# A routed-attention and tanh-shrink kernel on one core: order of the sums' product, of the weight checks, of the first two pairs and of the last flag, and how memory is handed over

## The chip, the cores and the metric

One core of a Trainium2 chip runs the whole program in one launch. The metric is the device time of one execution in microseconds (us), the median of the runs; lower is better. The engines are PE (TensorE, matrix products), DVE (VectorE), ACT (ScalarE) and POOL (GpSimd); SP only issues DMAs and waits. Every engine works through its own instructions in order and waits on semaphores for the others. A PE row in the trace gives matmuls; PEld rows are the weight loads beside them.

## The reference, cut to what matters

```
q, k, v: (4, 8, 768, 64) f32;  centroids: (8, 16, 64);  w_in: (512, 2048) f64;  w_out: (2048, 512) f64
assign  = argmax over 16 centroids of the normalised row . normalised centroid   (for q and for k)
scores  = q k^T / 8, kept only where q and k have the same cluster
attn    = exp(scores - max) / (sum + 1e-9);   x = attn v, heads side by side -> (3072, 512)
h = x w_in;   g = h - tanh(h);   out = g w_out          -> (3072, 512) f32
```

## The kernel before, in words

**Attention.** The 4 batches have 8 heads each, worked on in 16 pairs of heads (`pairs`, four to a batch, HP = 4). A pair is loaded (`load`: q, k and v on SP's queue), transposed (`turn`: PE into a PSUM tile, copied out by ACT or DVE), compared with the centroids (`similar`), given cluster codes (`route`, five DVE steps around a PE transpose), and its q codes go through DRAM (`publish`) to come back spread over the partitions (`spread`). Each pair has two halves of 384 queries, and each half has three steps (NS = 3) of two key tiles. A step is `score` (PE product, then ACT exp in PSUM), `select` (DVE: keep the exps whose codes match, tile `e`), and `value` (PE product into the PSUM tile `av`). `select` also lets POOL add the `e` tiles up into `sum` (L350, L354), except in the first half of the four pairs of batch 0, where PE does it (`early`).

**End of a half.** After the third step `total` (L383) multiplies `sum` by ones on PE (the sums' product, tile `den`, L391), has ACT copy `av` to `xT` (L396) and `den` to SBUF (L398), and POOL add it into `wholes` (L399). `divide` (three calls) makes the reciprocal on DVE (L405), multiplies `xT` by it (L408) and lets POOL add it into `inverses` (L409).

**Projections.** Batch 0 is projected by `plain_items` while its second halves and batch 1 are attended to. Batches 1 to 3 use a seven-product Strassen scheme (`strassen_items`): eight `up_pair` items (seven short PE products each, L595, DVE adds between, ACT tanh, POOL subtracts) and 21 `down_product` items (L637). Its factors are made once, kept in DRAM and streamed in by SP (`stream`, L536). While batch b+1 is attended to, batch b is projected; batch 3's items stand after the loop as the tail.

**Weights.** They come as 64-bit words. `weights_on` fetches a piece by POOL's queue and rounds it to f32 (ACT L120, DVE L121, L125, L128). Because the rounding holds only for values of some size, each half piece is read again later (`check_on`, SP, L728) and DVE reduces it to its least magnitude (`check_done`, L738): 64 checks.

**Order.** `steps` (L679) lists 96 attention steps. The loop emits for a step, in this order: the next pair's `similar`, `spread`, the next step's scores (`begin`), this step's `value`, at the end of a half `total`, and then the projection items of this step, in whose places (`between`) the list `todo` is spread out: the next step's selects, `turns`, divides, weight rounding, `route`, `publish`, the checks. Some steps have no item of their own: then all of `todo` is emitted at once; below these are called bare steps. In the Strassen stages the steps of a half are: a step with an `up_pair`, a bare step, a step with an `up_pair`.

**Memory.** `open_late` (L540) closes the pools of the first stages (weights, `g`, output and raw tiles) and opens the late ones on the same memory, among them `stream`, before step 48.

**End.** After the tail the checks, `wholes` and `inverses` become one flag (L854 to L868: six DVE steps, a PE transpose `pl`, a DVE reduction), which all engines load (L1017); a general path would follow if it were 0.

Of the kernel before, what the change touches and what calls it, by code (L numbers as in the profile page):

```python
# [30 lines left out]
F32 = mybir.dt.float32  # L31
# [7 lines left out]
P = 128  # L39
# [14 lines left out]
def kernel(  # L54
# [10 lines left out]
    nc = tc.nc  # L65
# [64 lines left out]
    def fast():  # L130
# [51 lines left out]
        def centroid_load():  # L182
            nc.scalar.dma_start(cen, centroids.rearrange("h c d -> (h c) d"))
# [128 lines left out]
        def spread(n: int, half: int):  # L312

            t = rows[n, half] = qbp.tile([P, 2, TB], BF16, name="row")
            nc.sync.dma_start(
                t.rearrange("p h n -> p (h n)"),
                q_codes[n][half].rearrange("h j p -> (h j p)").unsqueeze(0).to_broadcast([P, 2 * TB]),
            )
# [60 lines left out]
        def early(n: int, half: int):  # L379

            return n < HP and half == 0

        def total(n: int, half: int):  # L383

            b, p = pairs[n]
            s = sums.pop((n, half))
            ps = s
            if not early(n, half):
                ps = ps_f.tile([P, TB], F32, name="den", tag="f")
                for h in range(2):  # L390
                    nc.tensor.matmul(  # L391
                        ps[h * D : h * D + D], lhsT=ones, rhs=s[:, h], start=True, stop=True
                    )
            if half == 0:
                xT[n] = xp.tile([P, 2, TB], F32, name="xT")
            nc.scalar.copy(out=xT[n][:, half], in_=avs.pop((n, half)))  # L396
            t = dens[n, half] = sump.tile([P, TB], F32, name="den")
            nc.scalar.activation(out=t, in_=ps, func=ACT.Copy, bias=EPS)  # L398
            nc.gpsimd.tensor_tensor(out=wholes, in0=wholes, in1=t, op=ALU.add)  # L399
# [140 lines left out]
        def open_late():  # L540
            first.close()
            for name, bufs in (
                ("g", 1), ("diff", 1), ("u", 2), ("s", 2), ("th", 2), ("left", 1), ("du", 1), ("c", 4),
                ("stream", 3), ("raw", 1),
            ):
                late_pools[name] = cx.enter_context(tc.tile_pool(name=name + "_late", bufs=bufs))
            late_pools["G"] = late_pools["g"].tile([P, HF, 2, 2, TB], F32, name="G")
            late_pools["S1"] = late_pools["left"].tile([P, HF, TB], F32, name="S1")
            for n in range(2):
                fetch_factors(n)  # L550
# [192 lines left out]
        def begin(step):  # L743
            n, half, s = step
            for i in range(2):
                score(n, half, 2 * s + i)

        load(0)
        centroid_load()
        constants()  # L750
        for i in range(3):
            fetch()
        load(1)
        load(0, (2,))
        load(1, (2,))
        for n in range(2, HP):
            load(n, (0, 1, 2))
        turn(0, 0, nc.scalar)
        turn(0, 1, nc.vector)
        centroid_norms()  # L760
        similar(0)
        turn(1, 0, nc.scalar)
        route(0)
        publish(0)
        spread(0, 0)
        weights_on()
        begin(steps[0])
        weights_on()
        for i in range(2):
            select(*steps[0][:2], i)  # L770
        turn(1, 1, nc.scalar)
        similar(1)
        route(1)
        publish(1)


        fills = {HALF: (lambda: plain_items(0), HALF), 2 * HALF: (lambda: plain_items(1), 2 * HALF)}
        for b in range(1, B - 1):
            fills[2 * (b + 1) * HALF] = (lambda b=b: strassen_items(b), 2 * HALF)

        late, makers = [], []
        fill, whole, spent, since, over = [], 0.0, 0.0, 0, 1
        for at, (n, half, s) in enumerate(steps):
            b, p = pairs[n]
            following = steps[at + 1] if at + 1 < len(steps) else None
            after = steps[at + 2] if at + 2 < len(steps) else None
            if at == 4 * HALF:
                open_late()
            if at in fills:
                fill, over = fills[at][0](), fills[at][1]  # L790
                whole, spent, since = sum(it[0] for it in fill), 0.0, at
            if at == 2 * HALF:
                makers = [it for i in range(2) for it in up_maker(i)]
                makers += [it for i in range(2) for it in down_maker(i)]
            now = []
            part = (at - since + 1) / over
            while fill and (spent + fill[0][0] / 2 <= whole * part or part == 1):
                now.append(fill.pop(0))
                spent += now[-1][0]
            stages = ready.get(at, {})  # L800
            if 1 in stages:
                stages[1]()
            if after and after[2] == 0:
                spread(*after[:2])
            if following:
                begin(following)
            value(n, half, s)
            if s == NS - 1:
                total(n, half)
                late += [lambda n=n, half=half, i=i: divide(n, half, i) for i in range(HCH)]  # L810
                if half == 1:
                    load(n + (HP if n < 2 else 2), (2,) if n < 2 or n >= HP else ())

            todo = []
            if following:
                todo += [lambda i=i: select(*following[:2], 2 * following[2] + i) for i in range(2)]
            if 0 in stages:
                todo.append(stages[0])
            todo += late
            late = []  # L820
            todo += [weights_on] * (3 if HALF <= at < 2 * HALF else 1)
            if makers:
                share = -(-len(makers) // max(4 * HALF - 2 - at, 1))
                todo += makers[:share]
                makers = makers[share:]
            todo += [stages[i] for i in (2, 3) if i in stages]
            if late_pools:
                todo = [check_done] + todo + [check_on]
            slots = max(sum(it[1] for it in now), 1)
            place = iter(range(slots))  # L830

            def between():
                i = next(place)
                for it in todo[i * len(todo) // slots : (i + 1) * len(todo) // slots]:
                    it()

            if at in fills and late_pools:
                right_factors(b - 1)
            for it in now:
                it[2](between)  # L840
            if not now:
                between()
        for it in late:
            it()
        right_factors(B - 1)
        for it in strassen_items(B - 1):
            place = iter(range(9))
            it[2](lambda: (check_done(), check_on()) if next(place) == 0 else None)
        while waiting or (words == 2 and checked < 2 * len(PIECES)):
            check_done()  # L850
            check_on()


        for t, bound in ((inverses, MOST_INVERSE), (wholes, SUM_MOST)):  # L854
            nc.vector.tensor_scalar(out=t, in0=t, scalar1=bound, scalar2=None, op0=ALU.is_le)
# [10 lines left out]
        pl = ps_a.tile([1, P], F32, name="pl", tag="a")  # L866
        nc.tensor.transpose(out=pl, in_=fine, identity=ident)
        nc.vector.tensor_reduce(out=flag, in_=pl, axis=AX.X, op=ALU.min)  # L868


    def general():
# [180 lines left out]
```

## Time and profile before

| | |
|---|---|
| median of 3 runs (lowest, highest) | 1120.57 us (1119.27, 1124.29) |
| the profiled execution | 1122.21 us, its span 1120.4 us |
| mean granted TensorE clock | 0.971 |
| busy: PE, DVE, POOL, ACT | 91%, 55%, 49%, 27% of the span |

The profile comes from one execution; its span runs from the first to the last instruction of the program. A row of a timeline has the start in us, the duration in us, the engine, the line, the operation, the tiles as out<-in, and in square brackets how long the engine was idle before it and what ended that. A granted clock of 1.00 is TensorE's level of 2.4 GHz and 0.50 its level of 1.2 GHz; values between are stretches that hold both.

### The profile page before, as it was taken

How to read it: one execution, taken by the hardware profiler on the slowest of the kernel's cores; microseconds unless marked ns; L12 is line 12 of the kernel's file. 1: busy time of each engine (PE TensorE's matmuls, PEld its weight loads, DVE VectorE, ACT ScalarE, POOL GpSimd, SP SyncE). 2: the span in 40 equal slices, each digit the busy share in tenths (PEclk: the TensorE clock that was granted, in tenths of full speed). 3: DMA queues.
4: the chain of work that ended last, by engine and by line, in shares of the span. 5: the costliest groups of instructions: out<-in, count | busy, mean ns of one | idle time of the engine just before them, and what ended most of it. 6: DMA issues, size and time to landing. Idle time of an engine off the chain costs nothing.

```text
span 1120.4 us, 12005 instructions
## 1 busy us (share of the span) xinstructions
PE 1018.7 (91%) x4258; PEld 566.6 (51%) x4258; DVE 618.5 (55%) x1100; ACT 299.7 (27%) x458; POOL 552.9 (49%) x398
## 2 busy tenths in 40 slices
PE   3776999899999997889889999998889999999996
PEld 2332444344444442445446666544446766556885
DVE  3578899425776765465654544664635544544112
ACT  2343434213333332332223121222333121122000
POOL 1012354334545554475658634566668644356701
PEclk9888999999999999899999999999999999999998
DMA  9232354104244343423323343422332233334520
GB/s 226 75 106 78 90 170 134 45 17 120 77 129 135 122 158 104 131 78 109 114 92 122 116 129 124 128 90 94 87 134 95 94 115 104 122 127 138 191 99 31
DMA packets 101603, 124.68 MB, mean 111 GB/s; under 512 B 55328, under 2 KB 80928, under 8 KB 98848
## 3 DMA queue, kind: packets, MB, share of 16 engines
q1 hardware_dynamic: 94576, 100.73, 29.3%
q0 software_dynamic: 6816, 23.07, 6.3%
q8 instruction: 36, 0.59, 0.2%
q14 instruction: 31, 0.25, 0.1%
q10 hardware_dynamic: 144, 0.03, 0.0%
HBM read 102.79 MB, written 21.02 MB: 111 GB/s over the span
## 4 chain that ended last, share of the span: by engine, by line
PE 73%; DVE 11%; POOL 8%; DMA 3%; issue 3%; ACT 2%; SPq 0%; DVEq 0%; POOLq 0%; ACTq 0%
PE pu L595 19%; PE pd L637 19%; PE sc L327 9%; PE av L363 9%; PE o L437 7%; PE h L422 4%; POOL sum L354 4%; POOL G L586 3%; DVE e L341 2%; PE pt L248 2%; PE den L391 2%; PE sim L267 2%; DVE den L405 1%; DVE w_out L125 1%; PE den L372 1%
## 5 line engine op out<-in xcount | busy, mean ns | idle before, releaser
L354 POOL TENSOR_TENSOR sum<-sum,e 128x768 f32<-128x768 f32 x112 | 210.5, 1879 | 111.1 <-DVE e L341 106.9
L341 DVE SCALAR_TENSOR_TENSOR e<-row,code,sc 128x384 f32<-128x384 bf16 x384 | 211.5, 606 | 92.3 <-ACT sc L332 75.0
L332 ACT ACTIVATE sc<-sc 128x768 f32<-128x768 f32 x192 | 145.2, 790 | 255.9 <-PE sc L327 245.0
L637 PE MATMUL pd<-stream,G 128*128 128x256 f32 x864 | 193.3, 382 | 1.4 <-POOL G L586 1.4
L637 PEld LDWEIGHTS pd<-stream,G 128*128 128x128 f32 x864 | 162.3, 190 | 35.9 <-issue 9.6
L327 PE MATMUL sc<-t,t 64*128 64x384 f32 x768 | 160.5, 530 | 19.1 <-DVE e L341 16.4
L595 PE MATMUL pu<-xT,stream 128*128 128x384 f32 x384 | 145.7, 518 | 7.0 <-DMA stream<-up_factors 7.0
L363 PE MATMUL av<-e,vals 128*64 128x384 f32 x768 | 148.6, 509 | 0.0
L327 PEld LDWEIGHTS sc<-t,t 64*128 64x128 f32 x768 | 67.9, 191 | 96.0 <-issue 61.1
L586 POOL TENSOR_TENSOR G<-G,th 128x768 f32<-128x768 f32 x48 | 87.3, 1836 | 54.8 <-ACT th L585 54.8
L595 PEld LDWEIGHTS pu<-xT,stream 128*128 128x128 f32 x384 | 76.2, 202 | 68.5 <-issue 22.4
L595 PE MATMUL pu<-diff,stream 128*128 128x384 f32 x288 | 101.7, 486 | 0.8 <-DVE diff L561 0.8
L405 DVE RECIPROCAL den<-den 128x128 f32<-128x128 f32 x96 | 84.0, 918 | 18.0 <-POOL wholes L399 18.0
L363 PEld LDWEIGHTS av<-e,vals 128*64 128x64 f32 x768 | 47.5, 139 | 90.5 <-issue 89.4
L422 PE MATMUL h<-xT,w_in 128*128 128x384 f32 x256 | 88.4, 495 | 1.5 <-ACT den L398 1.3
L437 PE MATMUL o<-w_out,g 128*128 128x512 f32 x192 | 88.8, 610 | 0.0
L585 ACT ACTIVATE th<-G 128x768 f32<-128x768 f32 x48 | 39.4, 841 | 164.7 <-DVE G L581 164.7
L399 POOL TENSOR_TENSOR wholes<-wholes,den 128x384 f32<-128x384 f32 x32 | 31.8, 994 | 90.5 <-ACT den L398 90.5
L350 POOL TENSOR_TENSOR sum<-e 128x768 f32<-128x768 f32 x28 | 50.6, 1808 | 47.9 <-DVE e L341 47.9
L595 PEld LDWEIGHTS pu<-diff,stream 128*128 128x128 f32 x288 | 54.3, 190 | 38.3 <-DVE diff L561 1.4
L581 DVE TENSOR_TENSOR G<-pu,s 128x384 f32<-128x384 f32 x24 | 13.4, 557 | 105.8 <-PE pu L595 105.8
L653 POOL DMA_DIRECT2D out_dram<-c x36 | 19.9, 554 | 99.2 <-DVE c L648 96.9
(100 smaller groups left out, 913.9 us busy)
## 6 DMA issues: line engine op xcount, KB each, us to landing
stream<-up_factors SPq DMA_DIRECT2D x24, 896.0 KB, 5.5
stream<-down_factors SPq DMA_DIRECT2D x21, 1024.0 KB, 4.9
raw<-in_moe_w_in_dram POOLq DMA_DIRECT2D x16, 512.0 KB, 4.2
raw<-in_moe_w_out_dram POOLq DMA_DIRECT2D x16, 512.0 KB, 4.6
again<-in_moe_w_in_dram SPq DMA_DIRECT2D x32, 256.0 KB, 3.8
again<-in_moe_w_out_dram SPq DMA_DIRECT2D x32, 256.0 KB, 4.2
x<-in_q_dram SPq DMA_DIRECT2D x32, 192.0 KB, 5.7
x<-in_k_dram SPq DMA_DIRECT2D x32, 192.0 KB, 4.2
```

Source lines behind the costliest of these rows:

```text
L327: nc.tensor.matmul(sc[:, h, 0:TB], lhsT=turned[n, 1][r].rearrange("p a n -> p (a n)")[:, j * P : (j + 1) * P], rhs=turned[n, 0][r, half], ...
L332: nc.scalar.activation(out=sc[:, :, 0:TB], in_=sc[:, :, 0:TB], func=ACT.Exp, scale=SCALE)
L341: nc.vector.scalar_tensor_tensor(out=e[:, h], in0=rows[n, half][:, h], scalar=codes[n][:, 1, j // HCH, h, j % HCH : j % HCH + 1], in1=sc[: ...
L350: nc.gpsimd.tensor_tensor(out=s, in0=pair[:, 0], in1=pair[:, 1], op=ALU.add)
L354: nc.gpsimd.tensor_tensor(out=s, in0=s, in1=pair[:, i], op=ALU.add)
L363: nc.tensor.matmul(avs[n, half][h * D : h * D + D], lhsT=vals[n][:, h, j], rhs=e[:, i, h], start=(j == 0), stop=(j == NCH - 1),)
L405: nc.vector.reciprocal(out=t[:, c], in_=t[:, c])
L422: nc.tensor.matmul(h, lhsT=w_in[i][:, c, o * P : (o + 1) * P], rhs=xT[c][:, half], start=(c == 0), stop=(c == CD - 1),)
L437: nc.tensor.matmul(acc[sub], lhsT=gs[f % HF][:, f // HF, sub * P : (sub + 1) * P], rhs=w_out[f // FQ][:, f % FQ], start=(f == sequence[0]) ...
L586: nc.gpsimd.tensor_tensor(out=g[:, f].rearrange("p a n -> p (a n)"), in0=g[:, f].rearrange("p a n -> p (a n)"), in1=th.rearrange("p a n -> ...
L595: nc.tensor.matmul(ps, lhsT=streams[base + i][:, k_, c], rhs=right[which][c], start=(c == 0), stop=(c == CH - 1),)
L637: nc.tensor.matmul(ps, lhsT=left[:, i], rhs=t[:, i], start=(i == 0), stop=(i == HF - 1))
```

## The change

1. `total` is split. `take` has ACT copy `av` right after `value`. `total` itself (the sums' product, its copy, the POOL add) goes into `todo`, behind the selects and the turns, and the three divides into the next step's `todo`. The last pair of a batch keeps the old order in its second half (in batch 0 in both).
2. The two halves of a check part company: each step's `todo` now ends with two `check_done` and two `check_on`, where it began with one `check_done` and ended with one `check_on`. The late `raw` pool has 2 buffers for 1. The tail has no checks any more.
3. The late pools are opened with `reuse_waits="tile"`, so that a tile waits for the old tiles on whose memory it lies and not for the whole of the old pools.
4. Before the loop, pairs 0 and 1 are both transposed, routed and published, with four weight pieces rounded between them, where two were rounded and pair 1 followed the first selects; the loads of pairs 2 and 3 are emitted in another order, the centroids' load first, and the centroid norms before the second transpose.
5. The flag is made after the first two items of the tail, and the other items follow it.

```diff
+        def take(n: int, half: int):
+            if half == 0:
+                xT[n] = xp.tile([P, 2, TB], F32, name="xT")
+            nc.scalar.copy(out=xT[n][:, half], in_=avs.pop((n, half)))
+
         def total(n: int, half: int):
...
-            if half == 0:
-                xT[n] = xp.tile([P, 2, TB], F32, name="xT")
-            nc.scalar.copy(out=xT[n][:, half], in_=avs.pop((n, half)))
             t = dens[n, half] = sump.tile([P, TB], F32, name="den")
...
-                ("stream", 3), ("raw", 1),
+                ("stream", 3), ("raw", 2),
             ):
-                late_pools[name] = cx.enter_context(tc.tile_pool(name=name + "_late", bufs=bufs))
+                late_pools[name] = cx.enter_context(
+                    tc.tile_pool(name=name + "_late", bufs=bufs, reuse_waits="tile")
+                )
...
+        centroid_load()
         load(0)
-        centroid_load()
         constants()
         for i in range(3):
             fetch()
         load(1)
         load(0, (2,))
+        load(2)
         load(1, (2,))
+        load(3)
         for n in range(2, HP):
-            load(n, (0, 1, 2))
+            load(n, (2,))
         turn(0, 0, nc.scalar)
+        centroid_norms()
+        weights_on()
         turn(0, 1, nc.vector)
-        centroid_norms()
         similar(0)
+        weights_on()
         turn(1, 0, nc.scalar)
         route(0)
+        turn(1, 1, nc.scalar)
         publish(0)
         spread(0, 0)
+        similar(1)
         weights_on()
+        route(1)
         begin(steps[0])
+        publish(1)
         weights_on()
         for i in range(2):
             select(*steps[0][:2], i)
-        turn(1, 1, nc.scalar)
-        similar(1)
-        route(1)
-        publish(1)
...
             if s == NS - 1:
-                total(n, half)
-                late += [lambda n=n, half=half, i=i: divide(n, half, i) for i in range(HCH)]
+                take(n, half)
+                divides = [lambda n=n, half=half, i=i: divide(n, half, i) for i in range(HCH)]
+
+                if p == HP - 1 and (half == 1 or b == 0):
+                    total(n, half)
+                    late += divides
+                    divides = []
...
             todo += late
             late = []
+            if divides:
+                todo.append(lambda n=n, half=half: total(n, half))
+                late, divides = divides, []
...
             if late_pools:
-                todo = [check_done] + todo + [check_on]
+                todo += [check_done, check_done, check_on, check_on]
...
         right_factors(B - 1)
-        for it in strassen_items(B - 1):
-            place = iter(range(9))
-            it[2](lambda: (check_done(), check_on()) if next(place) == 0 else None)
-        while waiting or (words == 2 and checked < 2 * len(PIECES)):
-            check_done()
-            check_on()
-
+        tail = strassen_items(B - 1)
+        for it in tail[:2]:
+            it[2](lambda: None)
...
         nc.vector.tensor_reduce(out=flag, in_=pl, axis=AX.X, op=ALU.min)
+        for it in tail[2:]:
+            it[2](lambda: None)
```

## Rows read from the trace of the kernel before

**Rows 1.** The page's first part: busy time, share of the span, instructions.
```profile
PE 1018.7 (91%) x4258; PEld 566.6 (51%) x4258; DVE 618.5 (55%) x1100; ACT 299.7 (27%) x458; POOL 552.9 (49%) x398
```
**Rows 2.** Stages: length; busy PE, PEld, DVE, ACT, POOL; granted clock; DMA share, GB/s.
```profile
130.00:200.00 70.00, 63.23 (x230) 30.10 (x228) 66.38 (x104) 28.04 (x49) 33.38 (x30) 1.00 0.44 135
440.00:588.00 148.00, 126.70 (x486) 63.48 (x484) 80.20 (x150) 40.38 (x60) 85.13 (x58) 0.94 0.35 110
```
**Rows 3.** Waits of the whole run: total us, how often, the longest.
```profile
PE den L391 <- POOL sum L354: 20.6, 10, 3.3
PE sc L327 <- DVE e L341: 16.4, 16, 3.2
DVE smallest L738 <- DMA again<-in_moe_w_in_dram: 42.8, 11, 11.9
```
**Rows 4.** Timeline of a bare step and the half's end, and a later half's end.
```profile
495.08 1.58 ACT L585 ACTIVATE th<-G 128x768 f32<-128x768 f32 x2 [7.18 <-DVE G L581]
498.74 1.97 PE L327 MATMUL sc<-t,t 64*128 64x384 f32 x8 [0.82 <-DVE e L341]
505.42 0.91 PE L391 MATMUL den<-sum,ones 128*64 128x384 f32 x4 [3.27 <-POOL sum L354]
...
954.13 0.87 PE L391 MATMUL den<-sum,ones 128*64 128x384 f32 x4 [0.85 <-POOL sum L354]
```
**Rows 5.** Chain of waits, three whole up_pair items: start, duration, what.
```profile
471.80 10.92 PE pu L595 x28
...
542.12 9.23 PE pu L595 x28
...
833.75 10.92 PE pu L595 x28
```
**Rows 6.** Granted clock just behind the wait at 502 us (columns of group 2).
```profile
505.40:510.00 4.60, 4.58 (x11) 2.34 (x12) 0.00 (x0) 0.97 (x2) 0.99 (x1) 0.63 0.59 222
```
**Rows 7.** Timeline where the late pools are opened.
```profile
434.51 3.70 PE L437 MATMUL o<-w_out,g 128*128 128x512 f32 x8
...
440.26 0.56 POOL L446 DMA_DIRECT2D out_dram<-osb  x1
...
442.95 1.28 SPq L536 DMA_DIRECT2D stream<-up_factors  x3
...
448.14 4.48 PE L595 MATMUL pu<-xT,stream 128*128 128x384 f32 x8 [7.00 <-DMA stream<-up_factors]
```
**Rows 8.** Timeline before the loop.
```profile
17.93 0.47 PE L218 MATMUL pc<-ident,both 128*128 128x128 f32 x1 [4.83 <-DVE both L216]
...
30.89 2.19 DVE L341 SCALAR_TENSOR_TENSOR e<-row,code,sc 128x384 f32<-128x384 bf16 x4 [0.52 <-DMA row<-q_codes]
...
39.48 2.93 PE L327 MATMUL sc<-t,t 64*128 64x384 f32 x8
```
**Rows 9.** Timeline, divides of the first halves of pairs 0 and 1.
```profile
59.92 2.58 DVE L405 RECIPROCAL den<-den 128x128 f32<-128x128 f32 x3 [1.91 <-POOL wholes L399]
...
84.29 2.58 DVE L405 RECIPROCAL den<-den 128x128 f32<-128x128 f32 x3 [1.98 <-POOL wholes L399]
```
**Rows 10.** Timeline at the end of the weight rounding, DVE and PE.
```profile
197.25 0.42 DVE L121 TENSOR_SCALAR w_out<-raw 128x512 uint32<-128x512 uint32 x1
...
199.14 0.55 DVE L429 TENSOR_TENSOR g<-h,th 128x384 f32<-128x384 f32 x1
...
200.84 0.85 PE L248 MATMUL pt<-ident,x 128*128 128x128 f32 x6 [3.06 <-issue]
```
**Rows 11.** Timeline in the tail: end of its second item, then the flag.
```profile
981.25 0.56 DVE L581 TENSOR_TENSOR G<-pu,u 128x384 f32<-128x384 f32 x1 [0.27 <-PE pu L595]
...
1110.32 0.54 POOL L653 DMA_DIRECT2D out_dram<-c  x1 [2.92 <-DVE c L648]
...
1112.16 0.27 PE L867 MATMUL pl<-ident,fine 128*1 128x128 f32 x1 [2.60 <-DVE fine L865]
1112.46 0.28 DVE L868 TENSOR_REDUCE flag<-pl 1x1 int32<-1x128 f32 x1 [0.36 <-PE pl L867]
```

More of the change, by code (lines that the diff above doesn't have):

```diff
@@ L779, in fast @@
             fills[2 * (b + 1) * HALF] = (lambda b=b: strassen_items(b), 2 * HALF)
-        late, makers = [], []
+        late, divides, makers = [], [], []
         fill, whole, spent, since, over = [], 0.0, 0.0, 0, 1
```

## The prediction

> **What bounds the kernel now.** I read the page's busy shares first, then the busy times by stage, then the list of waits, and last the timeline where PE stood still. PE is busy 91% of the span, and no other engine over 55% [rows 1], so a saving counts only where it fills a hole in PE's row (or speeds its clock up); some 100 us of holes are there. The busy times by stage say where: between 130 and 200 us DVE is busy 66.4 of 70 us and PE waits for it, while in the first Strassen stage, 440 to 588 us, PE is busy 126.7 of 148 us with DVE and POOL little over half busy and the clock at 0.94 [rows 2]. There it is not work but order that costs: PE waits for POOL's sum in front of the sums' product, 20.6 us in ten waits, and for selects, 16.4 us in sixteen [rows 3]. Each term below is the hole that an edit can fill. The sum is made on the profiled execution, 1122.2 us with a span of 1120.4; it is 1.6 us above the median, 1120.6, and I carry the same difference over to the median.
>
> **The sums' product.** At 502 us PE has ended the half's values and waits 3.27 us for POOL's last add; then it goes on to an up_pair [rows 4]. Put behind the selects, the product comes third among that item's seven products, at 9.23/7 = 1.32 us each [rows 5], so about 4 us later, and the wait is covered with 0.7 us to spare. Of the 20.6 us, 0.85 stays (954 us, a batch's last half, which keeps its order [rows 4]) and about 0.8 lies in the DVE-bound stage below; 18.9 us go, in seven waits.
>
> The clock comes with it. Behind the wait at 502 us the granted clock is 0.63 over 4.6 us, so most of that time at 1.2 GHz [rows 6], and five of the up_pairs behind such waits take up to 10.92 us instead of 9.23 (the first and the last stand in [rows 5]): up to 1.7 us each, 8.4 at most. I take three of the five, 5.0 us, because one wait of two microseconds (before 542 us) was followed by the full 9.23 [rows 5]. The Trainium skill ("TensorE: Matmul & The Clock Gate", section "HAM oscillation — how this bites in real kernels") speaks against this: a PE that pauses a little but often between groups of matmuls can be moved to and fro between its two rates. By the page the 5.0 us would not come, by the 542 us row they do; the rest of the sum does not hang on it, and the case stands below as a rival.
>
> What is late next: DVE. The divides move one step on, and in the Strassen stages that is from a step followed by an up_pair to one followed by a bare step. In that up_pair DVE has seven adds of 0.56 us [rows 11], selects of 2.19 [rows 8], reciprocals of 2.58 [rows 9] and a multiply of one add's length, together 9.3 us, as long as the item's 9.23, with two checks besides. The adds can't run ahead of their products, so DVE ends behind PE. I walked the queue through (a product every 1.32 us, each DVE entry when its input and the entry before it are done) and get 1.25 us more lag than before. That lag is passed on: the tanh waits for DVE's add [rows 4], the bare step's exps stand behind the tanh on ACT, the selects behind the exps, and PE's scores behind the selects, which already wait 0.82 us there [rows 4]. Six bare steps follow such divides, so 6 x 1.25 = 7.5 us are lost; bounds 0 (DVE catches up) and 3.1 each (the whole divide shows). Two more steps emit the turns right behind the second select, whose PSUM slot they need: estimated 0.85 us each from the same walk, 1.7. The Strassen stages together: 18.9 + 5.0 - 7.5 - 1.7 = 14.7 us; bounds 18.9 - 18.6 - 1.7 = -1.4 and 18.9 + 8.4 = 27.3.
>
> **First halves of batch 0.** There DVE is in front of PE. Twice it waits for POOL's add into `wholes` before a divide, 1.91 and 1.98 us [rows 9], and with the divide a step later the add is long done: 3.9 us. Below it could be 0, when the q codes' way through DRAM (which follows in the same queue) ends last anyway.
>
> **The prologue.** First codes and the first row of codes come no sooner: the norms start earlier, but the second transpose now stands behind their product on PE (17.93 us before [rows 8], about 15.1 by the walk), and one weight rounding sits in front of its copy, so `similar` starts at 18.9 as now. What is saved is the second pair: before, its transposes, similarity and codes stood between the first selects (30.89) and the second scores (39.48) [rows 8]. Now they lie in holes of the first 31 us. Two more weight roundings and the second pair's codes come before the first selects, which I put at 33.9 instead of 30.9; the scores follow when the first select has freed its slot, at 35.1 instead of 39.5: 4.4 us. Bounds -3.8 (the holes on DVE are not there and the two roundings, 1.89 us each by [rows 10], show whole) and 6. The loads are only permuted: the two value loads that move back are wanted only in the loop. The order on SP's queue costs nothing.
>
> **The weight rounding that is now done early.** One costs 199.14 - 197.25 = 1.89 us of DVE [rows 10]. Two fewer remain in the stage of 130 to 200 us, which DVE fills: 3.8 us, and the hole of 3.06 us at 197.8 [rows 10], which is its backlog, is part of that. With the two short waits for the sums' product, 0.8, that is 4.6 us; bounds 0.8 and 6.
>
> **Memory by tile.** The first `stream` load is issued at 442.95, when the last output of batch 0 (issued at 440.26) has landed, and PE waits for it for 7.00 us, to 448.14 [rows 7]. By the pools' sizes the first stream tile lies on the old `g` tiles alone, which PE has read to the end at 434.51 + 3.70 = 438.2 [rows 7]. It can be issued some 4.8 us earlier, so the hole shrinks to 2.2 us, and the item behind it runs at full clock: 4.8 + 1.6 = 6.4 us. Bounds 0 (a tile's old readers are among the old pools' readers, so it can't wait longer than now) and 8.6.
>
> **The checks.** DVE waits 42.8 us for the input-weight checks alone, up to 11.9 at once [rows 3], in front of the selects; of PE's holes only what exceeds the usual 0.8 us in front of scores hangs on that, about 2 us in four places of the 16.4 [rows 3]. With the checks behind the selects I take 2.0; bounds 0 and 3. On SP the two new loads wait for DVE's reductions, and spreads and streams queue behind them; both are issued a step or more ahead, which hides it. In the tail PE does not wait for the checks; leaving them out gives nothing.
>
> **The flag.** Now it stands at the end: PE waits 2.60 us for DVE, the transpose takes 0.27, and the flag is there at 1112.74, 1.9 us after the last output's issue ended (1110.86) [rows 11]. Moved, it frees those 1.9 us. But PE meets the transpose right behind the second tail item, whose last DVE add ends at 981.81 [rows 11]; the six DVE steps come only then, so PE stands still for the same 2.6 + 0.27 us in a tail that PE bounds. Net loss 1.0 us; bounds +1.9 (the wait hidden) and -2.7 (a clock dip of 1.7 as well).
>
> **Sum.** 14.7 + 3.9 + 4.4 + 4.6 + 6.4 + 2.0 - 1.0 = 35.0 us: 1087.2 for the profiled execution, 1085.6 for the median.
>
> **Rivals.**
> - DVE takes the place of POOL: the lag is 3.1 us at each of the six bare steps (11.1 us more) and half the waits for the sums' product come back (9.5): 1106. For it: DVE's load equals the item's length. Against: DVE is busy little over half of that stage [rows 2]. 0.15.
> - The clock does not come back: 5.0 us gone, and a dip of 1.6 at six bare steps and at the flag, 11.2: 1102. For it: the page named above, and 10.92 at 471.8 after shorter waits [rows 5]. Against: the full 9.23 at 542 [rows 5]. 0.08.
> - The handing over does nothing (another old tile lies under the first stream tile, or the pools still wait as a whole): 6.4 us back, 1092. 0.10.
> - More than forecast: no DVE lag and no turn wait (9.2) and all clock dips gone (3.4): 1073. 0.12.
> - Slower: the checks. Their reductions now stand at the end of one step, so in front of the next step's selects, two instead of one. A bare step is short, and if the loads land late there, PE's scores wait with DVE. At the longest wait seen, 11.9 us [rows 3], six bare steps cost 71 us, and the time is 1157; it decides from 35.0/6 = 5.8 us each, where the gain is eaten. Against: a load has a whole step to land. 0.06, a third of that near no change.
>
> The forecast has 0.49, with its own range 1077 to 1094. The range 1070 to 1107 takes in the first four rivals and leaves out the slower case and the far end of the better one. A measurement here can tell about 0.5%, 5.6 us, from no change: faster 0.94, same 0.02, slower 0.04.
>
> **What would show it.** The waits of `den` on `sum` fall from 20.6 to a few us; the bare steps' waits for selects rise to about 2 us; the first `pu` starts within 3 us of the values before it; the second scores start at 35 us; a hole of nearly 3 us with the transpose `pl` stands near 981 us less what was gained before it; the last output's issue is followed at once by the load of the flag. Large waits for `again`, or den waits in new places, would make it wrong.

## The result and the profile after

| | before | after |
|---|---|---|
| median of 4 runs (lowest, highest) | 1120.05 us (1119.27, 1124.29) | 1080.41 us (1078.31, 1084.10) |
| ratio, 95% interval | | 0.964 (0.961 to 0.968) |
| the profiled execution, its span | 1122.21, 1120.4 us | 1080.79, 1078.9 us |
| mean granted TensorE clock | 0.971 | 0.982 |

The change saves 39.6 us; 35.0 were forecast. The first part of the page after, and of its waits the lines that answer to [rows 1] and [rows 3]:

```profile
PE 1007.2 (93%) x4258; PEld 557.9 (52%) x4258; DVE 622.4 (58%) x1100; ACT 300.7 (28%) x458; POOL 551.6 (51%) x398
```
```profile
PE sc L327 <- DVE e L341: 22.7, 13, 5.5
PE pl L879 <- DVE fine L877: 6.7, 1, 6.7
PE den L396 <- POOL sum L354: 0.5, 1, 0.5
```

The waits of `den` on `sum` fell from 20.6 us in ten to 0.5 in one. PE's longest hole behind the prologue is now the flag's, 6.7 us. DVE's waits for `again`, 42.8 and 24.0 us before, are not in the list any more.

To lay the two executions side by side I cut them at the first `av` product of the same attention steps (counted from 0). Busy times of the two Strassen stages with `up_pair` items (steps 50 to 60 and 72 to 84), columns as in [rows 2], of the kernel before and then of the kernel after:

```profile
467.62:587.20 119.58, 106.37 (x399) 53.16 (x397) 66.02 (x123) 33.43 (x50) 73.73 (x50) 0.96 0.30 95
708.81:846.09 137.28, 124.42 (x483) 62.14 (x481) 79.46 (x150) 40.76 (x61) 84.58 (x58) 0.96 0.33 103
```
```profile
446.19:555.27 109.08, 103.56 (x399) 50.80 (x397) 67.02 (x132) 34.74 (x52) 75.57 (x51) 0.98 0.42 133
673.83:800.87 127.04, 121.61 (x482) 60.23 (x481) 78.18 (x152) 41.84 (x62) 84.30 (x57) 0.99 0.39 124
```

The first two numbers of a row, length and PE busy, say most. Their difference is PE's idle time: it fell from 13.21 and 12.86 us to 5.52 and 5.43, by 15.1 in all. PE's busy time for the same products fell by 5.6, with the granted clock up from 0.96 to 0.98 and 0.99. DVE and POOL do about the same work as before.

What stands in the Strassen stages now (timeline, as [rows 4]):

```profile
471.26 1.63 ACT L589 ACTIVATE th<-G 128x768 f32<-128x768 f32 x2 [8.30 <-DVE G L585]
474.92 2.51 PE L327 MATMUL sc<-t,t 64*128 64x384 f32 x8 [1.79 <-DVE e L341]
483.96 0.87 PE L396 MATMUL den<-sum,ones 128*64 128x384 f32 x4
497.44 0.87 PE L248 MATMUL pt<-ident,x 128*128 128x128 f32 x6 [0.89 <-ACT t L255]
509.59 1.97 PE L327 MATMUL sc<-t,t 64*128 64x384 f32 x8 [0.63 <-DVE e L341]
540.22 1.97 PE L327 MATMUL sc<-t,t 64*128 64x384 f32 x8 [1.80 <-DVE e L341]
720.92 2.70 PE L327 MATMUL sc<-t,t 64*128 64x384 f32 x8 [2.02 <-DVE e L341]
723.56 2.39 PE L363 MATMUL av<-e,vals 128*64 128x384 f32 x8
785.82 1.96 PE L327 MATMUL sc<-t,t 64*128 64x384 f32 x8 [1.42 <-DVE e L341]
```

`den` meets no wait. Four of the six bare steps wait 1.4 to 2.0 us for a select, two 0.63; 0.82 stood in [rows 4]. Behind the waits at 474.92 and 720.92 PE runs at its lower level for a moment (eight `sc` products in 2.51 and 2.70 us for 1.97; the granted clock is 0.58 from 477.5 to 480 us and 0.63 from 723.6 to 726), behind those at 540.22 and 785.82 it does not. Such dips do not fall in the same places in every execution: of these four waits none to two are followed by one in the seven profiled executions with this order (two in the kernel after, u_pools, flag_end, flag_later and flag_split, one in best, none in u_prologue), so stages of like code differ by some 1.6 us for each. The whole `up_pair` at 772.25, on the chain of waits, takes the full rate's 9.23 us, where 10.92 stood twice in [rows 5]:

```profile
772.25 9.23 PE pu L599 x28
```

Before the loop, in the first halves and where memory is handed over (timeline, as [rows 7 to 9]):

```profile
32.82 2.19 DVE L341 SCALAR_TENSOR_TENSOR e<-row,code,sc 128x384 f32<-128x384 bf16 x4 [0.42 <-DMA row<-q_codes]
34.10 2.93 PE L327 MATMUL sc<-t,t 64*128 64x384 f32 x8 [5.47 <-DVE e L341]
...
59.04 2.57 DVE L407 RECIPROCAL den<-den 128x128 f32<-128x128 f32 x3
...
427.69 0.56 POOL L448 DMA_DIRECT2D out_dram<-osb  x1
428.51 2.85 PE L599 MATMUL pu<-xT,stream 128*128 128x384 f32 x8
```

The second scores start at 34.10 for 39.48 us, right behind the first select, as forecast. The reciprocals stand without the waits of 1.91 and 1.98 us, the second (at 81.37) as the one shown. The first `pu` follows at once, at full rate; the last output of batch 0 was issued 0.8 us before it, so its stream load did not wait for that output to land.

In the tail (timeline, as [rows 11]): the flag's steps, and the last output.

```profile
934.19 4.08 POOL L590 TENSOR_TENSOR G<-G,th 128x768 f32<-128x768 f32 x2 [3.36 <-ACT th L589]
934.57 2.04 DVE L868 TENSOR_TENSOR wholes<-wholes,inverses 128x384 f32<-128x384 f32 x1
936.53 1.79 DVE L870 TENSOR_SCALAR smallest<-smallest 128x64 f32<-128x64 f32 x1
938.35 0.99 POOL L623 TENSOR_TENSOR S<-G 128x384 f32<-128x384 f32 x1
938.35 1.07 DVE L873 TENSOR_TENSOR wholes<-wholes,smallest 128x64 f32<-128x64 f32 x1
940.06 0.37 PE L879 MATMUL pl<-ident,fine 128*1 128x128 f32 x1 [6.66 <-DVE fine L877]
940.23 4.54 PE L599 MATMUL pu<-xT,stream 128*128 128x384 f32 x8
...
1070.57 0.42 DVE L652 TENSOR_TENSOR c<-pd,du 128x256 f32<-128x256 f32 x1 [3.03 <-PE pd L641]
```

The hole is there, but 6.66 us long, not the 2.60 of [rows 11]. Eight `pu` products behind it take 4.54 us where eight take 2.85 at 428.51; the granted clock is 0.62 from 940 to 945 us. From step 95 to the end of the span it is 174.2 us, where it was 168.7.

### The profile page after: what moved, and what is told of

Its sections match the earlier page's. It is cut to its first block, busy times and chain, and to the rows that moved or that the text cites. A ratio compares the mean times of both kernels' runs of the same rounds, so it can differ in the third digit from the quotient of the medians.

```text
span 1078.9 us, 11996 instructions
## 1 busy us (share of the span) xinstructions
PE 1007.2 (93%) x4258; PEld 557.9 (52%) x4258; DVE 622.4 (58%) x1100; ACT 300.7 (28%) x458; POOL 551.6 (51%) x398
## 4 chain that ended last, share of the span: by engine, by line
PE 75%; DVE 10%; issue 7%; POOL 3%; SPq 2%; ACT 2%; DMA 1%; POOLq 0%; DVEq 0%; ACTq 0%
PE pu L599 19%; PE pd L641 14%; PE sc L327 12%; PE av L363 11%; PE o L439 8%; PE h L424 6%; DVE e L341 3%; SPq L238 2%; PE den L396 2%; PE pt L248 2%; PE sim L267 1%; DVE den L407 1%; DVE w_out L125 1%; PE den L372 1%; POOL G L661 1%
## 5 line engine op out<-in xcount | busy, mean ns | idle before, releaser
L354 POOL TENSOR_TENSOR sum<-sum,e 128x768 f32<-128x768 f32 x112 | 207.9, 1856 | 94.4 <-DVE e L341 90.1
L327 PE MATMUL sc<-t,t 64*128 64x384 f32 x768 | 156.6, 519 | 25.1 <-DVE e L341 22.7
L599 PE MATMUL pu<-xT,stream 128*128 128x384 f32 x384 | 138.9, 498 | 0.0
L599 PEld LDWEIGHTS pu<-xT,stream 128*128 128x128 f32 x384 | 71.7, 192 | 59.3 <-issue 11.2
L350 POOL TENSOR_TENSOR sum<-e 128x768 f32<-128x768 f32 x28 | 53.6, 1916 | 80.1 <-DVE e L341 80.1
L424 PEld LDWEIGHTS h<-xT,w_in 128*128 128x128 f32 x256 | 47.6, 192 | 45.1 <-issue 8.7
L411 POOL TENSOR_TENSOR inverses<-inverses,den 128x384 f32<-128x384 f32 x32 | 41.5, 1297 | 37.6 <-DVE den L407 36.7
```

The source lines that it names most:

```text
L327: nc.tensor.matmul(sc[:, h, 0:TB], lhsT=turned[n, 1][r].rearrange("p a n -> p (a n)")[:, j * P : (j + 1) * P], rhs=turned[n, 0][r, half], ...
L350: nc.gpsimd.tensor_tensor(out=s, in0=pair[:, 0], in1=pair[:, 1], op=ALU.add)
L354: nc.gpsimd.tensor_tensor(out=s, in0=s, in1=pair[:, i], op=ALU.add)
L424: nc.tensor.matmul(h, lhsT=w_in[i][:, c, o * P : (o + 1) * P], rhs=xT[c][:, half], start=(c == 0), stop=(c == CD - 1),)
L599: nc.tensor.matmul(ps, lhsT=streams[base + i][:, k_, c], rhs=right[which][c], start=(c == 0), stop=(c == CH - 1),)
```

## The experiments

Each kernel is the kernel after with one edit, unless it says otherwise, and was timed against the kernel before on the same chip (median there 1121.3 to 1122.1 us).

| kernel | median (lowest, highest), us | ratio to before, 95% |
|---|---|---|
| u_total: product at once | 1111.25 (1109.31, 1114.37) | 0.991 (0.990 to 0.993) |
| divide_same: divides at once | 1105.37 (1103.44, 1107.44) | 0.986 (0.984 to 0.988) |
| divide_later: product at once, divides late | 1109.97 (1107.08, 1110.27) | 0.989 (0.987 to 0.991) |
| only_total: before with part 1 alone | 1096.94 (1095.28, 1098.53) | 0.979 (0.977 to 0.980) |
| checks_first: reductions ahead of selects | 1096.02 (1091.66, 1099.02) | 0.977 (0.974 to 0.979) |
| u_checks: part 2 undone, flag at the end | 1078.41 (1077.84, 1080.15) | 0.962 (0.961 to 0.964) |
| u_pools: pools handed over whole | 1087.62 (1084.72, 1091.77) | 0.970 (0.967 to 0.972) |
| u_prologue: part 4 undone | 1085.57 (1084.27, 1085.83) | 0.968 (0.966 to 0.970) |
| flag_end: flag after the tail | 1073.06 (1071.32, 1074.84) | 0.956 (0.954 to 0.958) |
| flag_later: whole flag behind 18 items | 1077.33 (1075.82, 1079.03) | 0.961 (0.958 to 0.963) |
| flag_split: transpose two items later | 1071.77 (1071.14, 1073.16) | 0.956 (0.954 to 0.958) |
| best: flag_split, some products at once | 1067.38 (1065.49, 1072.55) | 0.953 (0.951 to 0.955) |

### The product and the divides

**u_total.** The sums' product again stands right behind the values, the divides in the same step.

```diff
-                if p == HP - 1 and (half == 1 or b == 0):
+                if True:
```

> The changed kernel with the sums' product back right behind the values (divides in the same step's list), all else as changed. Theory: this part carries the Strassen stages' gain and the 3.9 us of the first halves: waits of the sums' product on POOL's sum back to 15-20 us, the bare steps' wait of scores for selects back to about 0.8 us, up_pairs behind the long waits at 10.5-10.9 us; time 1080.4 + 18.9 (waits) + 5 (clock) + 3.9 (first halves) - 4 (lag given back) = about 1104. Rival: the gain of these stages came from the checks' new place; then the time stays within 6 us of 1080.

It cost 31 us, more than was expected. Eight waits of 3.15 to 3.20 us are back in front of `den`, and the scores of four bare steps wait no more than 0.69 us for a select again (timeline, PE):

```profile
455.05 1.16 PE L396 MATMUL den<-sum,ones 128*64 128x384 f32 x4 [3.15 <-POOL sum L354]
483.90 1.97 PE L327 MATMUL sc<-t,t 64*128 64x384 f32 x8 [0.69 <-DVE e L341]
```

That alone is 25 us, more than the 18.9 counted in the kernel before, and the clock falls with them: the same stages are 28 us longer than in the kernel after; the stage of the weight rounding (steps 11 to 21) is 3 us shorter.

**only_total.** The kernel before with the diff's `take`, the deferred `total` and the late divides, and nothing else.

> The kernel before with the first part of the change alone (product deferred, divides one step later). Theory: the waits for POOL's sum and most clock dips go: 1120.6 - 17 to 24 = 1097 to 1104. Rival: without the checks' new place the selects come too late behind the checks' loads and the bare steps take half of it back: 1110.

Part 1 alone saves 24 us, the upper end of what was expected. The waits of `den` are gone with it. Its cuts: 4.6 us in the first halves, 17.1 in the two Strassen stages with `up_pair` items, 4.3 in those with `down_product` items, for which the forecast had no term.

**divide_same.** The product stays deferred, its divides follow it in the same step.

```diff
             if divides:
                 todo.append(lambda n=n, half=half: total(n, half))
-                late, divides = divides, []
+                todo += divides
+                divides = []
```

> The changed kernel with the divides directly behind the deferred sums' product in the same step's list, not one step later. Theory: the step's delay is what spares DVE the wait for POOL's add (ACT copy 0.5 us and POOL add 1.0 us behind the product); without it DVE stands in front of the up_pair's adds for 1.5 us or more in the Strassen stages and 2 us in the first halves, but the bare steps' waits of 1.4 to 2.0 us fall to 0.8: net 1080 to 1086. Rival: the divides in front of a bare step were the worse place, and without them there the time falls to 1076.

A miss: 25 us slower than the kernel after. The Strassen stages with `up_pair` items hardly changed (109.8 and 127.9 us for 109.1 and 127.0). The largest loss, 12.9 us, is where batch 1 is projected (steps 21 to 47): 214.6 us for 201.7; the first halves lose 5.4 (77.9 for 72.5), and the rest is spread over the other stages. DVE waits 81.2 us in 31 places for POOL's add into `wholes`, where it was 8.2 in four. Its timeline in steps 21 to 47, POOL, DVE and PE:

```profile
300.16 1.00 POOL L401 TENSOR_TENSOR wholes<-wholes,den 128x384 f32<-128x384 f32 x1 [1.22 <-ACT den L400]
301.19 2.58 DVE L407 RECIPROCAL den<-den 128x128 f32<-128x128 f32 x3 [4.20 <-POOL wholes L401]
307.91 2.79 PE L248 MATMUL pt<-ident,x 128*128 128x128 f32 x12 [2.71 <-issue]
```

The reciprocal stands at the head of DVE's queue while product, copy and POOL's add are still to come: DVE idles 4.20 us, and PE then 2.71.

**divide_later.** The other half alone: product right behind the values, divides a step later.

```diff
                 divides = [lambda n=n, half=half, i=i: divide(n, half, i) for i in range(HCH)]
+                total(n, half)
...
-                    total(n, half)
...
-                todo.append(lambda n=n, half=half: total(n, half))
```

> The changed kernel with the sums' product right behind the values, but the divides one step later as changed. With the changed kernel (1080), the one with both early (1111) and the one with only the divides early (1105) this fills the table of four. Theory: in the Strassen stages PE's waits for POOL's sum come back as in the kernel with both early (3.15 us, eight times, some 28 us), the first halves keep their gain of 6 us, 200 to 440 us stays without holes: 1105. Rival: with the divides away from DVE's queue POOL's sums end sooner and the waits are half as long: 1094.

Slower by 5 us than expected. It keeps the gain of the first halves (71.8 us) and loses nothing in steps 21 to 47, but has both kinds of wait in the Strassen stages (timeline, PE):

```profile
476.03 1.97 PE L327 MATMUL sc<-t,t 64*128 64x384 f32 x8 [1.87 <-DVE e L341]
482.66 1.55 PE L396 MATMUL den<-sum,ones 128*64 128x384 f32 x4 [3.22 <-POOL sum L354]
```

So the two orders belong together:

| medians, us | divides in the same step | divides a step later |
|---|---|---|
| product at once | 1111 | 1110 |
| product deferred | 1105 | 1080 |

The late product takes PE's wait for POOL away but puts the divides' inputs later; the late divides take DVE's wait for those inputs away. Either alone brings 1 to 6 us of the 31.

### The weight checks

**checks_first.** Both reductions ahead of the selects, the two buffers kept.

```diff
-                todo += [check_done, check_done, check_on, check_on]
+                todo = [check_done, check_done] + todo + [check_on, check_on]
```

> The changed kernel with the two reductions of the checks at the head of the list, in front of the selects, and the two loads at its end; two buffers and two checks a step as changed. Theory: the place behind the selects was worth about 4 us (down stages, where DVE waited up to 11.9 us for a load in front of the selects): 1084 to 1086, with DVE waits for the loads in front of selects and PE waits for selects behind them. Rival: only the waiting of one buffer cost anything, and two buffers cure it: 1080.

It cost 15.6 us, some three times what was expected. DVE waits for `again` once more, and the bare steps' scores with it (waits of the whole run, then the timeline):

```profile
DVE smallest L742 <- DMA again<-in_moe_w_in_dram: 17.4, 9, 4.9
DVE smallest L742 <- DMA again<-in_moe_w_out_dram: 17.0, 10, 4.8
```
```profile
477.00 2.52 PE L327 MATMUL sc<-t,t 64*128 64x384 f32 x8 [3.22 <-DVE e L341]
```

**u_checks.** One reduction ahead and one load behind, one buffer, checks in the tail, all as before; the flag at the end, so it is to be compared with flag_end.

```diff
-                ("stream", 3), ("raw", 2),
+                ("stream", 3), ("raw", 1),
...
-                todo += [check_done, check_done, check_on, check_on]
+                todo = [check_done] + todo + [check_on]
...
```

> The changed kernel with the checks wholly as before (one buffer, one reduction in front of the selects, one load at the end, the last ones in the tail) and so with the flag at the very end; to be held against the one with the flag at the end (1073). Theory: DVE waits for the loads in front of selects come back and cost PE 5 us in the down stages and some in bare steps: 1078 to 1082. Rival: as in the kernel before, where PE waited little for that: 1074 to 1075.

It came out within what was expected, 5.3 us over flag_end, the intervals apart; 2.0 were forecast. Most of it, 4.1 us, lies in the second Strassen stage with `up_pair` items (129.55 us for 125.41), and there it is mostly clock: PE's busy time for the same products is 3.4 us longer, with a granted clock of 0.97 for 1.00, and its idle time 0.8. With the reduction in front of the selects, four bare steps wait 2.19 us for a select, and behind each of the four PE slows down, as in only_total, which has this order of the checks too; in flag_end the same four wait 1.4 to 2.0 us, and behind two of them it does. One of the four (timeline):

```profile
722.15 2.22 PE L327 MATMUL sc<-t,t 64*128 64x384 f32 x8 [2.19 <-DVE e L341]
724.29 2.83 PE L363 MATMUL av<-e,vals 128*64 128x384 f32 x8
```

### The pools and the prologue

**u_pools.** The late pools wait for the old ones as a whole.

```diff
-                    tc.tile_pool(name=name + "_late", bufs=bufs, reuse_waits="tile")
+                    tc.tile_pool(name=name + "_late", bufs=bufs, reuse_waits="pool")
```

> The changed kernel with the late pools waiting as whole pools again. Theory: the first stream load is issued when the last batch-0 output has landed, PE waits 7 us in front of the first up_pair and runs it partly at 1.2 GHz: 1080.4 + 7.7 = 1088. Rival: the earlier finish of the divides had made the stream early anyway; then no difference (1080).

The hole is back, behind a stream load that again follows the last output (timeline):

```profile
431.97 0.56 POOL L448 DMA_DIRECT2D out_dram<-osb  x1
434.67 1.28 SPq L538 DMA_DIRECT2D stream<-up_factors  x3
439.81 4.38 PE L599 MATMUL pu<-xT,stream 128*128 128x384 f32 x8 [6.96 <-DMA stream<-up_factors]
```

Steps 47 to 49 take 30.4 us for 22.7: the handing over is worth 7.7 us.

**u_prologue.** The order before the loop as it was, the diff's block undone.

> The changed kernel with the old order before the loop (two roundings, pair 1 behind the first selects). Theory: step 0's values 5.4 us later, and two more weight roundings of 1.9 us in the stage where DVE is full: 1080.4 + 5.4 + 2 to 3.8 = 1088 to 1090. Rival: all 13 us gained up to step 21 come from here: 1093; other rival: DVE catches up later and only 2 us remain: 1082.

It cost 5.2 us by the medians, and 1085.57 is below the 1088 to 1090 expected; the forecast had 4.4 for the second pair and 3.8 for the two roundings. Some 4.2 us of it lie before the loop (32.3 us from the first matmul to the first values, for 28.1 in flag_later and flag_split, whose first load lands as late). The stage of the weight rounding takes 109.5 us, inside the 107.0 to 110.4 of all kernels with the product deferred, so what the two early roundings are worth there is not shown.

### The flag

**flag_end.** All tail items, then the flag, without checks in the tail.

```diff
-        for it in tail[:2]:
+        for it in tail[:]:
...
-        for it in tail[2:]:
-            it[2](lambda: None)
```

> The changed kernel with the flag back at the very end. Theory: the flag in the tail cost more than it saved: a hole of 6.66 us in PE and half clock behind it (1.7 us) against about 2 us at the end, so 1080.4 - 5.5 = 1075. Rival: the hole is made up later in the tail and the end's 2 us are lost: 1082.

7.3 us faster than the kernel after: the flag's place alone cost that. Its tail takes 167.9 us where the kernel before, with the checks in it, took 168.7.

**flag_later.** The whole flag after 18 of the tail's items, among the `down_product` items.

```diff
-        for it in tail[:2]:
+        for it in tail[:18]:
...
-        for it in tail[2:]:
+        for it in tail[18:]:
```

> The changed kernel with the whole flag chain, PE transpose in place, behind the tenth down product of the tail (18 items instead of 2), where POOL has no elementwise work. Theory: three of the six DVE steps took 2.04, 1.79 and 1.07 us instead of 0.56, 0.19 and 0.23 because POOL's subtracts ran beside them; away from POOL they take their old times and PE's hole is 2.5 to 3 us: 1080.4 - 4 (hole) - 1.7 (clock) = 1075. Rival: DVE's steps are slow because of their waits on one another in mid-program; then the hole stays at 6 to 7 us and the time at 1080.

Slower than expected by 2.3 us, but what it was built for shows: away from POOL's subtracts the DVE steps take 0.56 and 0.19 us, and PE waits 2.60 us as in [rows 11] (timeline). The clock dip, which the expectation took to go as well, came behind this shorter hole too: the granted clock is 0.67 from 1027 to 1032 us.

```profile
1025.65 0.56 DVE L868 TENSOR_TENSOR wholes<-wholes,inverses 128x384 f32<-128x384 f32 x1
1026.12 0.19 DVE L870 TENSOR_SCALAR smallest<-smallest 128x64 f32<-128x64 f32 x1
1027.21 0.37 PE L879 MATMUL pl<-ident,fine 128*1 128x128 f32 x1 [2.60 <-DVE fine L877]
```

**flag_split.** The DVE steps there, PE's transpose two items later.

```diff
-        for it in tail[:2]:
+        for it in tail[:18]:
...
         nc.vector.tensor_reduce(out=fine, in_=wholes, axis=AX.X, op=ALU.min)
+        for it in tail[18:20]:
+            it[2](lambda: None)
         pl = ps_a.tile([1, P], F32, name="pl", tag="a")
...
-        for it in tail[2:]:
+        for it in tail[20:]:
```

> As the one with the flag behind 18 tail items, but two more down products stand between the DVE steps and the PE transpose. Theory: the hole in PE disappears (under 0.5 us) and the 2 us at the end are saved as well: 1072 to 1073, the fastest of all. Rival: the end does not shorten without the flag (the last output's landing sets it): 1075.

As expected. The tail takes 165.6 us for 167.9 in flag_end and 174.2 in the kernel after; the timed intervals of flag_split and flag_end overlap.

**best.** flag_split, and the product right behind the values for the 12 steps in which DVE is full.

```diff
-                if p == HP - 1 and (half == 1 or b == 0):
+                if (p == HP - 1 and (half == 1 or b == 0)) or HALF <= at < 2 * HALF:
...
```

> The kernel with the split flag, and the sums' product of batch 0's second halves (steps 12 to 17) right behind the values again. Theory: in that stage the deferral costs 3 us (from step 11 to step 21 the changed kernel takes 108.7 us, the one with the product behind the values 105.7), because DVE is full and its subtract, late behind the weight rounding, holds the PSUM slot that the product and the next projection want: 1071.8 - 3 = 1069. Rival: the 3 us come from the weight rounding alone and stay: 1072.

It beats both kernels: 53.9 us under the kernel before, 13.0 under the kernel after by the medians. Its stage of steps 11 to 21 takes 105.7 us for 107.3 in flag_split. The two ratios overlap, so that its second edit helps is shown by the stage and not by the timing. PE passes the flag without a wait (timeline):

```profile
1020.05 0.56 DVE L868 TENSOR_TENSOR wholes<-wholes,inverses 128x384 f32<-128x384 f32 x1
1025.76 0.27 PE L881 MATMUL pl<-ident,fine 128*1 128x128 f32 x1
```

## Why the prediction was right

The sum was right because its steps were, mostly, and in part by luck: mis-sized terms of opposite sign cancelled. Without part 5 the time is 1073.06 (flag_end), outside the forecast's own range of 1077 to 1094, though inside the whole range. Forecast and stage by stage measurement, in us saved:

| term | forecast | measured |
|---|---|---|
| Strassen stages, with the checks | 14.7 + 2.0 | 26.8 |
| first halves of batch 0 | 3.9 | 5.5 |
| prologue | 4.4 | 4.1 |
| stage of the weight rounding | 4.6 | 2.1 |
| memory by tile | 6.4 | 7.7 |
| flag | -1.0 | -5.5 |
| steps 21 to 47; landing of the first load, which differs by execution | 0 | -0.4; 1.3 |
| sum | 35.0 | 41.6 (spans: 41.5) |

**The sums' product.** The step was right: the waits went (u_total, only_total). The two stages with `up_pair` items gave 20.7 us, the step in front of them 1.2, the stages with `down_product` items 4.9, for which the forecast had no term; why they became shorter was not separated. In the first two PE's idle time fell by 15.1 us where 18.9 - 7.5 - 1.7 + 2.0 = 11.7 were forecast. The mis-sized term is "1.25 us more lag than before" at six bare steps: four of them wait 0.6 to 1.2 us more than the 0.82 of [rows 4], two wait 0.2 less, together 3.4 us and not 7.5. The two turns wait 0.89 each, as estimated (0.85). With the 1.3 us in front of the scores at 726.57 in the kernel before, which went too, the rows give 18.9 - 3.4 - 1.8 + 1.3 = 15.0.

The clock's part, 5.6 us by PE's busy time, agrees with the 5.0 taken, but not by the forecast's reckoning: all five slow `up_pair` items became fast, not three (10.92, 10.83, 10.47, 10.92 and 10.92 us for 9.23, together 7.9), and the two new dips at bare steps took some 3.3 back.

**First halves, prologue.** The waits for `wholes` in the first halves are gone; of the 5.5 us there 1.2 is PE's busy time (60.90 us before, 59.72 after, at a granted clock of 0.87 and 0.94), for which no term stood. The second scores start at 34.1, where 35.1 was put; the first load landed 1.3 us earlier in this execution. u_prologue confirms part 4, but as one sum.

**The weight rounding.** The two early roundings were counted (3.8; no run shows them alone), and the deferral itself was taken to help by 0.8 where DVE is full. It costs there, and it is here that `den` waits "in new places", which the prediction had named as a sign against it: put behind the selects, `den` waits for the slot that DVE's subtract `g` holds, and `h` too (timeline, PE, kernel after):

```profile
141.81 0.87 PE L396 MATMUL den<-sum,ones 128*64 128x384 f32 x4 [0.79 <-DVE g L431]
144.29 2.85 PE L424 MATMUL h<-xT,w_in 128*128 128x384 f32 x8 [1.60 <-DVE g L431]
```

u_total, divide_later and best, which have the product at once there, take 104.7 to 105.7 us for this stage; the kernel after took 108.7 and its relatives with the product deferred 107.0 to 110.4.

**Memory by tile.** The forecast left 2.2 us of the hole; none was left.

**The checks.** "2.0" was too small: 5.3 by u_checks. The reading under it was also off: from step 48 on, where the checks run, PE's waits for a select in the kernel before exceed the usual 0.82 us in three places (0.95, 1.32, 1.14), by 1.0 us and not by 2. From step 47 to the end u_checks has 2.3 us more of PE idle than flag_end and 3.1 more of PE busy for the same products. What the forecast left out is the second part, the clock dips behind the bare steps' waits, four in u_checks and two in flag_end.

**The flag.** The step "PE stands still for the same 2.6 + 0.27 us" failed. At the end of the kernel before the six DVE steps ran alone; in the tail's middle three of them ran beside POOL's subtracts and the add behind them and took 4.90 us together (2.04, 1.79, 1.07) where they took 0.98 before, in this timeline of the kernel before:

```profile
1110.59 0.56 DVE L856 TENSOR_TENSOR wholes<-wholes,inverses 128x384 f32<-128x384 f32 x1
1111.07 0.19 DVE L858 TENSOR_SCALAR smallest<-smallest 128x64 f32<-128x64 f32 x1
1111.29 0.23 DVE L861 TENSOR_TENSOR wholes<-wholes,smallest 128x64 f32<-128x64 f32 x1
```

The difference, 3.9 us, is nearly the whole of 6.66 - 2.60 = 4.06. The clock dip of 1.7 behind it, which stood at the end of the bounds, came too (4.54 for 2.85). At the end 2.5 us were freed, from the last `c` to the span's end (10.4 to 7.9), where 1.9 was taken. flag_later shows the cause: away from POOL's subtracts the hole is 2.60 again.

**The rivals.** DVE did not take POOL's place: no wait of `den` for POOL's sum came back in the Strassen stages. The clock rival came true in a small part, at two bare steps (some 1.6 us each: `sc` 2.51 for 1.97, `av` 2.39 for 1.51) and at the flag, and the four waits of 1.4 to 2.0 us between groups of products never slowed a whole `up_pair`. So the to and fro that the Trainium skill describes ("TensorE: Matmul & The Clock Gate", section "A second HAM failure mode: psum-queue depth-cycling", which follows the section named in the prediction) shows here as single dips. The mean granted clock rose from 0.971 to 0.982. The handing over did its work. The slower rival, the checks, has its mechanism seen in checks_first, at 1.4 us a bare step (3.22 for 1.79) and not the 5.8 from which it decides; in the kernel after the loads landed in time. The better rival's number, 1073, is what flag_end reached (1073.06), but not by its mechanism: DVE's lag and the turns' waits stayed in part (3.4 and 1.8 us), and the stages with `down_product` items, the first halves and the memory gave more than was forecast for them.

## What to carry to other kernels

A product that waits for a slow engine's sum can go behind other work of its queue, but then what consumes its result has to go a step later too; where the engine between them is already full, as DVE is in the stage of the weight rounding, the product is better left in its place. A short chain at the end of a program that is moved into a busy stretch is to be priced by what runs beside it there, not by its rows at the end, and the product that closes it belongs some items behind the steps that feed it.

## What the hardware showed that was not expected

DVE steps with both inputs in SBUF (the memory on the chip that the engines share), and a `tensor_scalar` of 128x64, waited inside their own duration while POOL's `tensor_tensor` ran: 2.04 us for 0.56, 1.79 for 0.19, 1.07 for 0.23. POOL's pair of subtracts took 4.08 us beside them for the 3.58 at 472.19 in the same kernel, some 0.5 more, about one such DVE step:

```profile
472.19 3.58 POOL L590 TENSOR_TENSOR G<-G,th 128x768 f32<-128x768 f32 x2 [1.88 <-ACT th L589]
```

The reduction `fine` behind them took its usual 0.55 us, with POOL's next subtract at work at the same time:

```profile
939.42 0.99 POOL L624 TENSOR_TENSOR G<-G 128x384 f32<-128x384 f32 x1
939.45 0.55 DVE L877 TENSOR_REDUCE fine<-wholes 128x1 f32<-128x384 f32 x1
```

The Trainium skill ("SBUF — State Buffer", section "Who interferes with whom") has this rule: a DVE step with two SBUF inputs, or one in a mode that uses both ports, and a GpSimd step that reads SBUF exclude each other, so that the one that starts first holds the other up for its whole length; a reduction on DVE is not held up. The trace agrees in each of the four steps and in POOL's, though it does not show the mode of the `tensor_scalar`. That rule, set against POOL's rows at that place, would have put the flag's DVE steps behind the subtracts and not beside them.
